# Full-array scores and joined sums in a fused chunk attention and ReGLU kernel: block 2's attention moved into output units, a reordered start, and stores from another queue

## The chip, the cores and the metric

The kernel runs on one core of one Trainium2 chip. The metric is device time in microseconds (us) of that core. A number called "span" is the profiled execution, from its first to its last instruction; a run's time is about 1.7 us more than its span. Profiles name the engines PE (TensorE, matmuls), PEld (its weight loads, which overlap matmuls), DVE (VectorE), ACT (ScalarE), POOL (GpSimd) and SP (SyncE). "PEclk" is the granted clock of TensorE as a share of full speed.

## The reference, cut to what matters

Attention over chunks of 32 tokens (each chunk sees 16 tokens to its left, 8 to its right and 8 memory rows), then a gated feed-forward network. Batch 4, 8 heads of 64, 768 tokens: 3072 tokens of width 512; the hidden width is 1536.

```python
def _attn_ref(q, k, v, mem_k, mem_v):          # cut
    for c in range(nc):
        k_full = np.concatenate([mem_k, k_ctx], axis=2)
        v_full = np.concatenate([mem_v, v_ctx], axis=2)
        scores = scale * np.matmul(q_c, k_full.transpose(0, 1, 3, 2))
        scores = scores - np.max(scores, axis=-1, keepdims=True)
        a = np.exp(scores)
        a = a / (np.sum(a, axis=-1, keepdims=True) + 1e-09)
        out[:, :, c_start:c_end] = np.matmul(a, v_full)

def _moe_ref(x, w_gate, w_val, w_out):
    gate = np.maximum(x @ w_gate, 0.0)
    val = x @ w_val
    return gate * val @ w_out
```

## The kernel before

The tokens are cut into 8 blocks of 384. A block goes through attention, four pairs of heads one after the other, and leaves a transposed tile `xT`. Then it goes through the feed-forward network in 15 units: 12 gate/value units of 8 matmuls of 384 columns, and 3 output units of 12 matmuls of 512 columns. TensorE is to be busy all the time, so the attention of block n+1 is cut into pieces that stand between the units of block n. Everything else hangs on this interleaving.

One pair of heads in the kernel before: 8 score matmuls on half of the array each, sums of the exponentials by a matmul with ones, values on half of the array, a reciprocal made by ACT as exp(-ln(x)), and one multiply on DVE.

```python
    def score_mms(n, hp, sc, start):
        kT, qT = kTs[n], qTs[n]
        for i in range(NQ):                    # NQ = 4 parts of QB = 96 tokens
            for hh in range(2):
                s = slice(D * hh, D * hh + D)  # D = 64: half the array
                nc.tensor.matmul(sc[:, hh, QB * i:QB * i + QB], lhsT=kT[s, i, hp, :], rhs=qT[s, i, hp, :],
                                 start=start, stop=start or i == NQ - 1)
    # ... step_s: score_mms, then three Exp with the mask as bias -> ex

    def step_d(n, hp):                         # sums, L253
        ex = exs[n, hp]
        parts = [(0, 1, 1), (1, NQ, 0)] if n % 2 == 0 else [(0, NQ - 1, 0), (NQ - 1, NQ, 2)]
        for i0, i1, kind in parts:
            for hh in range(2):
                nc.tensor.matmul(xs[D * hh:D * hh + D, QB * i0:QB * i1], lhsT=ones[:, kind, :],
                                 rhs=ex[:, hh, i0:i1, :], start=True, stop=True)

    def step_l(n, hp):
        nc.scalar.activation(xs, xs, ACT.Ln, scale=1.0 / 64.0)

    def step_e(n, hp):
        rinv = rpool.tile([128, TB], F32, name="rinv")
        nc.scalar.activation(rinv, xs, ACT.Exp, scale=-1.0, bias=mln64)
        rinvs[n, hp] = rinv

    def step_v(n, hp):                         # values, L268
        ex, vw = exs.pop((n, hp)), vwins[n % 2]
        for i in range(NQ):
            for hh in range(2):
                nc.tensor.matmul(xo[D * hh:D * hh + D, QB * i:QB * i + QB], lhsT=vw[:, i, 2 * hp + hh, :],
                                 rhs=ex[:, hh, i, :], start=True, stop=True)

    def step_m(n, hp):
        nc.vector.tensor_tensor(out=x_of(n)[:, hp, :], in0=xo, in1=rinvs.pop((n, hp)), op=ALU.mult)
```

A gate/value unit and the loop that interleaves. The units share two buffers of accumulators (`f_ps`), so unit u+2 can't start before DVE has made `gv` of unit u.

```python
    def ffn_close(n):
        for ps, m in units[n]:
            gr = grpool.tile([128, TB], F16, name="gr")
            nc.scalar.activation(gr, ps[:, 0, 0:TB], ACT.Relu)
            nc.vector.tensor_tensor(out=gvs[n][:, m, :], in0=ps[:, 1, 0:TB], in1=gr, op=ALU.mult)

    def run(order, n, first, gap, wait, turn_at):
        s_at = [first + gap * hp for hp in range(HP)]
        for u, (b, x) in enumerate(order):
            if n < NB:
                pieces(n, [("m", hp) for hp in range(HP) if u == s_at[hp] + wait + 1])
                now = [hp for hp in range(HP) if u == s_at[hp] + wait]
                unit(b, x, between(n, [(w, hp) for hp in now for w in "dlv"]))
                pieces(n, [("e", hp) for hp in now])
                pieces(n, [("s", hp) for hp in range(HP) if u == s_at[hp]])
            # ... turn_dma(n + 1) at turn_at

    run([(1, m) for m in range(6)] + [(0, NDC + t) for t in range(NT)] + [(1, m) for m in range(6, NDC + NT)],
        2, 6, 2, 2, 9)
    for n in range(2, NB):
        loads(n + 2)
        run([(n, u) for u in range(NDC + NT)], n + 1, 0, 3, 2, 9)
```

Block 0 has nothing to stand between. Its keys and queries are cast, turned on TensorE ("turns", `kq_ps`) and copied. Block 1 is turned the same way. From block 2 on, transposing DMAs (`turn_dma`) give `kT` and `qT`.

The softmax here doesn't subtract the row's maximum and nothing guards it: scores larger than these inputs give would overflow.

## Time and profile before

The time before is 251.81 us (median of 4 runs beside the changed kernel, 250.84 to 252.85); the profiled run's span is 249.3 us.

| stage of the span before | from, us | to, us |
|---|---|---|
| start, block 0's attention, its first units | 0 | 28.94 |
| block 1's turns | 28.94 | 35.98 |
| units 7 to 11 of block 0, with block 1's values | 35.98 | 45.52 |
| block 1's units, block 0's output units, with block 2's attention | 45.52 | 86.36 |
| block 2's units, with block 3's attention | 86.36 | 113.51 |
| blocks 3 to 6, 27.15 us each | 113.51 | 222.11 |
| block 7's units and the end | 222.11 | 249.3 |

The head of the page of the kernel before: the span, then per engine the busy us, the share of the span and the number of instructions.

```profile
span 249.3 us, 4594 instructions
PE 235.5 (94%) x1850; PEld 127.1 (51%) x1850; DVE 81.3 (33%) x162; ACT 127.6 (51%) x275; POOL 87.4 (35%) x116
```

TensorE is the limit. The chain of waits of the kernel before, in a steady block (start, us, what ran; the chain is followed back from the last instruction):

```profile
113.51 1.30 PE f_ps L285 x8
114.81 0.28 PE sc_ps L217 x8
115.09 2.06 PE f_ps L285 x12
117.14 0.29 PE xs_ps L253 x4
117.43 0.17 PE xo_ps L268 x8
117.60 2.06 PE f_ps L285 x12
119.66 0.28 PE sc_ps L217 x8
...
132.89 7.77 PE o_ps L310 x36
```

Only TensorE is on it. A unit takes 1.30 us for 8 matmuls, so 163 ns each; three output units take 7.77; the next block starts at 140.66. A pair of heads comes every 4.85 us (119.66 - 114.81). What a pair costs TensorE beyond the units is to be seen in the timeline of one pair in the kernel before (start, us, engine, line, what, and in brackets how long the engine was idle before it and what released it):

```profile
117.05 0.56 DVE L292 TENSOR_TENSOR gv<-f_ps,gr 128x384 f16<-128x384 f32 x1 [1.12 <-ACT gr L291]
117.07 0.14 PEld L253 LDWEIGHTS <-ones 128*64 128x64 f16 x4 [0.32 <-issue]
117.07 0.36 PE L253 MATMUL xs_ps<-ex,ones 128*64 128x96 f16 x4
...
118.39 0.49 ACT L291 ACTIVATE gr<-f_ps 128x384 f16<-128x384 f32 x1 [0.45 <-PE f_ps L285]
...
118.78 0.57 ACT L261 ACTIVATE rinv<-xs_ps,mln 128x384 f32<-128x384 f32 x1
...
118.92 0.56 DVE L292 TENSOR_TENSOR gv<-f_ps,gr 128x384 f16<-128x384 f32 x1 [1.31 <-ACT gr L291]
119.39 0.55 DVE L272 TENSOR_TENSOR xT<-xo_ps,rinv 128x384 f16<-128x384 f32 x1
```

The weights of the half-array groups are not loaded ahead: PEld stands idle 0.32 us before the sums. The page "TensorEngine Tiling (Array Packing)" of the Trainium skill (section Key Properties) says that a change of tiling mode drains the array, and this trace agrees with it.

Only two waits of TensorE at its matmuls are large after the start. They are in the waits of the kernel before (engine, line, waited for: us in total, times, longest):

```profile
PE sc_ps L217 <- DMA qT<-q16n: 4.0, 1, 4.0
...
PE f_ps L285 <- DVE gv L292: 0.8, 1, 0.8
```

The first is the wait for block 2's transposed queries, which ends at 60.20. After it the clock is low, as the windows of the kernel before show (stretch, its length, busy us of PE, PEld, DVE, ACT, POOL; then PEclk, DMA share, GB/s):

```profile
57.00:60.50 3.50, 0.30 (x8) 0.32 (x8) 0.00 (x0) 0.00 (x0) 1.54 (x2) 0.94 2.12 159
60.50:64.00 3.50, 3.50 (x16) 1.25 (x11) 0.00 (x0) 1.20 (x3) 1.99 (x3) 0.57 2.08 198
```

A clock of 0.57 over 3.5 us costs 3.5 x 0.43 = 1.5 us. The page "TensorE: Matmul & The Clock Gate" (section on the HAM clock gate) says that TensorE falls to half its clock after an idle window of about 3.4 us and needs about as long at work to return; here a wait of 4.03 us was followed by 3.5 us at about half clock.

### The profile page before, as it was taken

How to read it: one execution, taken by the hardware profiler on the slowest of the kernel's cores; microseconds unless marked ns; L12 is line 12 of the kernel's file. 1: busy time of each engine (PE TensorE's matmuls, PEld its weight loads, DVE VectorE, ACT ScalarE, POOL GpSimd, SP SyncE). 2: the span in 40 equal slices, each digit the busy share in tenths (PEclk: the TensorE clock that was granted, in tenths of full speed). 3: DMA queues.
4: the chain of work that ended last, by engine and by line, in shares of the span. 5: the costliest groups of instructions: out<-in, count | busy, mean ns of one | idle time of the engine just before them, and what ended most of it. 6: DMA issues, size and time to landing. Idle time of an engine off the chain costs nothing.

```text
span 249.3 us, 4594 instructions
## 1 busy us (share of the span) xinstructions
PE 235.5 (94%) x1850; PEld 127.1 (51%) x1850; DVE 81.3 (33%) x162; ACT 127.6 (51%) x275; POOL 87.4 (35%) x116
## 2 busy tenths in 40 slices
PE   7798999993999999999999999999999999999994
PEld 3454655551455455545554455545554555555541
DVE  3454564430044043411442043503441145203410
ACT  4173369322286277635774467626763577423321
POOL 8988759523974920195007800320000000000000
PEclk9799999998999999999999999999999999999998
DMA  7999999999999998099938997095701200030012
GB/s 170 157 191 194 175 186 172 199 152 183 163 188 142 189 205 152 0 127 192 137 52 50 187 120 147 8 158 115 88 0 45 85 0 3 0 126 3 0 42 84
DMA packets 113726, 28.57 MB, mean 115 GB/s; under 512 B 100170, under 2 KB 110634, under 8 KB 113706
## 3 DMA queue, kind: packets, MB, share of 16 engines
q0 software_dynamic: 86896, 15.17, 76.5%
q1 hardware_dynamic: 26394, 12.73, 22.6%
q10 hardware_dynamic: 416, 0.39, 0.6%
q8 instruction: 14, 0.23, 0.4%
q14 instruction: 6, 0.05, 0.1%
HBM read 31.15 MB, written 6.29 MB: 150 GB/s over the span
## 4 chain that ended last, share of the span: by engine, by line
PE 74%; DMA 15%; POOL 6%; issue 2%; SPq 1%; ACT 0%; POOLq 0%
PE f_ps L285 43%; PE o_ps L310 25%; DMA wv<-in_moe_w_val_dram 8%; DMA qT<-q16n 4%; DMA wo<-in_moe_w_out_dram 3%; PE xs_ps L253 3%; PE sc_ps L217 3%; POOL vwin L135 3%; PE xo_ps L268 2%; SPq L203 1%; POOL wg L169 1%; POOL wv L169 1%; POOL q16n L156 1%; POOL rk L126 0%; POOL memv L138 0%
## 5 line engine op out<-in xcount | busy, mean ns | idle before, releaser
L292 DVE TENSOR_TENSOR gv<-f_ps,gr 128x384 f16<-128x384 f32 x96 | 53.4, 557 | 130.9 <-ACT gr L291 130.9
L285 PE MATMUL f_ps<-xT,wg 128*128 128x384 f16 x384 | 79.4, 327 | 0.8 <-DVE gv L292 0.8
L285 PE MATMUL f_ps<-xT,wv 128*128 128x384 f16 x384 | 79.3, 327 | 0.0
L291 ACT ACTIVATE gr<-f_ps 128x384 f16<-128x384 f32 x96 | 47.1, 491 | 44.5 <-PE f_ps L285 42.5
L310 PE MATMUL o_ps<-wo,gv 128*128 128x512 f16 x288 | 65.2, 385 | 0.0
L135 POOL DMA_DIRECT2D vwin<-in_v_dram x32 | 28.8, 909 | 58.2 <-PE xo_ps L268 55.7
L285 PEld LDWEIGHTS <-wg 128*128 128x128 f16 x384 | 35.0, 97 | 25.6 <-issue 1.1
L285 PEld LDWEIGHTS <-wv 128*128 128x128 f16 x384 | 35.6, 98 | 23.4 <-issue 0.2
L310 PEld LDWEIGHTS <-gv 128*128 128x128 f16 x288 | 28.3, 99 | 34.0 <-issue 1.9
L313 ACT COPY o_sb<-o_ps 128x512 f32<-128x512 f32 x24 | 14.0, 585 | 46.1 <-PE o_ps L310 46.1
L239 ACT ACTIVATE ex<-sc_ps,bias 128x256 f16<-128x256 f32 x84 | 33.5, 476 | 6.5 <-PE sc_ps L217 6.5
L135 POOL DMA_DIRECT2D k<-in_k_dram x24 | 21.4, 906 | 6.2 <-DMA wo<-in_moe_w_out_dram 2.5
L272 DVE TENSOR_TENSOR xT<-xo_ps,rinv 128x384 f16<-128x384 f32 x32 | 17.7, 553 | 17.3 <-ACT rinv L261 14.4
L156 POOL DMA_DIRECT2D q16n<-in_q_dram x24 | 18.7, 801 | 8.0 <-DMA vwin<-in_v_dram 5.1
L257 ACT ACTIVATE xs_ps<-xs_ps 128x384 f32<-128x384 f32 x32 | 15.3, 479 | 11.8 <-PE xs_ps L253 10.2
L261 ACT ACTIVATE rinv<-xs_ps,mln 128x384 f32<-128x384 f32 x32 | 18.4, 576 | 0.2
L217 PE MATMUL sc_ps<-qT,kT 64*128 64x96 f16 x192 | 8.4, 208 | 4.0 <-DMA qT<-q16n 4.0
L268 PE MATMUL xo_ps<-ex,vwin 128*64 128x96 f16 x256 | 11.0, 207 | 0.7 <-DVE xT L272 0.7
L253 PE MATMUL xs_ps<-ex,ones 128*64 128x96 f16 (+1 forms) x128 | 11.4, 258 | 0.0
L217 PEld LDWEIGHTS <-kT 64*128 64x128 f16 x192 | 4.9, 95 | 11.9 <-issue 11.9
L198 DVE CAST kq<-kq_ps 128x896 f16<-128x896 f32 x8 | 8.7, 1091 | 6.5 <-PE kq_ps L189 6.4
L268 PEld LDWEIGHTS <-vwin 128*64 128x64 f16 x256 | 8.7, 110 | 2.8 <-issue 2.4
(50 smaller groups left out, 67.8 us busy)
## 6 DMA issues: line engine op xcount, KB each, us to landing
out_dram<-o_sb SPq DMA_DIRECT2D x24, 256.0 KB, 2.2
vwin<-in_v_dram POOLq DMA_DIRECT2D x24, 120.0 KB, 5.2
q16n<-in_q_dram POOLq DMA_DIRECT2D x24, 96.0 KB, 6.9
k<-in_k_dram POOLq DMA_DIRECT2D x18, 120.0 KB, 6.8
wo<-in_moe_w_out_dram POOLq DMA_DIRECT2D x3, 512.0 KB, 9.7
wg<-in_moe_w_gate_dram POOLq DMA_DIRECT2D x4, 256.0 KB, 7.4
wv<-in_moe_w_val_dram POOLq DMA_DIRECT2D x4, 256.0 KB, 8.0
rk<-in_k_dram POOLq DMA_DIRECT2D x3, 224.0 KB, 8.2
```

The source lines that it names most:

```text
L135: pool_dma(dsts[p][NMEM + m0:NMEM + m1, i], src)
L156: pool_dma(q16s[n][:, i], src)
L217: nc.tensor.matmul(sc[:, hh, QB * i:QB * i + QB], lhsT=kT[s, i, hp, :], rhs=qT[s, i, hp, :], start=start, stop=start or i == NQ - 1)
L239: nc.scalar.activation(ex[:, :, :, s], src, ACT.Exp, scale=SCALE, bias=bias[:, g:g + 1])
L253: nc.tensor.matmul(xs[D * hh:D * hh + D, QB * i0:QB * i1], lhsT=ones[:, kind, :], rhs=ex[:, hh, i0:i1, :], start=True, stop=True)
L261: nc.scalar.activation(rinv, xs, ACT.Exp, scale=-1.0, bias=mln64)
L268: nc.tensor.matmul(xo[D * hh:D * hh + D, QB * i:QB * i + QB], lhsT=vw[:, i, 2 * hp + hh, :], rhs=ex[:, hh, i, :], start=True, stop=True)
L272: nc.vector.tensor_tensor(out=x_of(n)[:, hp, :], in0=xo, in1=rinvs.pop((n, hp)), op=ALU.mult)
L285: nc.tensor.matmul(ps[:, a, 0:TB], lhsT=(wg, wv)[a][:, f, 128 * m:128 * m + 128], rhs=xTs[n][:, f, :], start=(f == 0), stop=(f == NFC - 1))
L291: nc.scalar.activation(gr, ps[:, 0, 0:TB], ACT.Relu)
L292: nc.vector.tensor_tensor(out=gvs[n][:, m, :], in0=ps[:, 1, 0:TB], in1=gr, op=ALU.mult)
L310: nc.tensor.matmul(o_ps, lhsT=gvs[n][:, m, 128 * t:128 * t + 128], rhs=wo[:, m, :], start=(m == 0), stop=(m == NDC - 1))
```

## The change

The intent: fewer and fuller matmuls per pair of heads. From block 1 on the values tile holds `[v | ones]` (128 columns), so one matmul gives values (rows 0 to 63) and sums (rows 64 to 127). From block 3 on the queries are spread block-diagonally, so 4 full-array matmuls of 192 columns replace 8 half-array ones. (Smaller edits, not shown: the order of loads, and `rpool` with 2 buffers instead of 4.) Around it: the casts of the start go ahead of the copies, unit 2 of block 0 takes the score banks, block 2's scores move from places 6, 8, 10 and 12 of the order of units to 11, 12, 14 and 15, so that its attention stands in the output units of blocks 0 and 1, the columns of ones are written by DVE memsets, and stores are issued by ACT instead of SP. The result tile `X` has one buffer of two banks.

```diff
 def step_s(n, hp):
+        if n < 3:
+            score_mms(n, hp, sc, True)
+        else:
+            for i in range(NQ):
+                nc.tensor.matmul(sc[:, i // 2, 192 * (i % 2):192 * (i % 2) + 192], lhsT=kTs[n][:, i, hp, :],
+                                 rhs=qbds[n % 2][:, i, hp].rearrange("p h m -> p (h m)"), start=True, stop=True)
 ...
-    def step_d(n, hp):              # sums by ones
 ...
+    def step_v(n, hp):
+        ex, vw, X = exs.pop((n, hp)), vwins[n % 2], first["X"]
+        for i in range(NQ):
+            for hh in range(2):
+                nc.tensor.matmul(X[:, hh, QB * i:QB * i + QB], lhsT=vw[:, i, 2 * hp + hh, :],
+                                 rhs=ex[:, hh, i, :], start=True, stop=True)
+        ln = rpool.tile([D, 2, TB], F32, name="ln")
+        nc.scalar.activation(ln, X[D:128, :, 0:TB], ACT.Ln, scale=1.0 / 64.0)
+    def step_e(n, hp):
+        rinv = rpool.tile([D, 2, TB], F32, name="rinv")
+        nc.scalar.activation(rinv, lns.pop((n, hp)), ACT.Exp, scale=-1.0, bias=mln64[0:D, :])
     def step_m(n, hp):
-        nc.vector.tensor_tensor(out=x_of(n)[:, hp, :], in0=xo, in1=rinvs.pop((n, hp)), op=ALU.mult)
+        for hh in range(2):
+            nc.vector.tensor_tensor(out=x_of(n)[D * hh:D * hh + D, hp, :], in0=first["X"][0:D, hh, 0:TB],
+                                    in1=rinv[:, hh, :], op=ALU.mult)
 ...  # stores
-        sp(out[row0:row0 + 128, :], o_sb)
+        act_dma(out[row0:row0 + 128, :], o_sb)
 ...  # start
+        for hp in range(2):
+            cast(0, hp, dve_copy)
+            cast(1, hp, act_copy)
+        turn_pe(0, 0)
+        turn_copy(0, 0)
 ...  # behind block 0's first value multiply, and again behind gv of unit 2
+        one_words(1, 0, 128, 0, NQ, ONE)
+        one_words(1, 96, 128, NQ - 1, NQ, 0)
+        one_words(1, 96, 120, NQ - 1, NQ, ONE)
 ...  # block 1
-    sums(1, 0)
     step_s(1, 2)
     ffn_unit(0, 7)
-    sums(1, 1)
     step_s(1, 3)
-    values(1, 0)
+    value(1, 0)                     # value = step_v, step_e, step_m in a row
     ffn_unit(0, 8)
-    values(1, 1)
-    sums(1, 2)
+    value(1, 1)
 ...  # run: where the scores stand is now a tuple, the place of "m" is unchanged
+                pieces(n, [("m", hp) for hp in range(HP) if u == at[hp] + wait + 1])
+                now = [hp for hp in range(HP) if u == at[hp] + wait]
+                unit(b, x, [lambda w=("v", hp): pieces(n, [w]) for hp in now])
 ...
-    run([(1, m) for m in range(6)] + [(0, NDC + t) for t in range(NT)] + [(1, m) for m in range(6, NDC + NT)],
-        2, 6, 2, 2, 9)
+    run([(1, m) for m in range(NDC)] + [(b, NDC + t) for b in range(2) for t in range(NT)],
+        2, (11, 12, 14, 15), 2, 13)
+    pieces(2, [("m", 3)])
```

## The prediction

> **What bounds it now.** TensorE: the page has PE busy 94% of the 249.3 us span; the chain of waits is 74% PE. From 86 us on a block takes 27.15 us (chain: 86.36, 113.51, 140.66): 96 matmuls of 163 ns are 15.6, output units 7.77, so the four head pairs cost 3.7, 0.93 each: scores 0.27, sums 0.19, values 0.27, two gaps of 0.10 (timeline). The Trainium skill (TensorEngine Tiling, Key Properties) says changing the tiling mode drains the array; the trace agrees, weight loads idle 0.32 us before such groups. Elsewhere PE loses 1.7 us waiting for the second key cast (timeline, 6.3 to 8.0), 0.8 at 22.7 (waits: f_ps on gv), 4.0 at 56 to 60 waiting for block 2's transpose (waits: sc_ps on DMA qT) and then about 1.6 at half clock (windows: 0.57 in 60.5 to 64).
>
> **What changes, costed.**
> 1. Blocks 3 to 7: 4 score matmuls of 192 columns (estimate 83 ns each, from 163 per 384) and 8 of 96 giving values and sums together (estimate 42 to 60 ns; not in this trace). No sums, no gaps: 0.67 to 0.85 for 0.93. ACT grows: Ln and Exp on 64x768 take about 0.81 (as the 128x768 Exp) and 0.9, from 0.48 and 0.58; DVE multiplies twice. ACT is then about 80% full, PE waits up to 0.1. Block about 26.4; five blocks: -3.5 us (0 to -5).
> 2. Start: the second turn no longer waits; heads 4 to 7 land near 9.5. About -2. Given back: memsets of ones columns (1024 words, estimate 1.1 us from 0.27 for 256) sit on DVE between block 0's first two multiplies (+0.6) and behind gv of unit 2 (+1.0). The 0.8 wait goes. Net about -1.
> 3. Block 1 values: one X buffer, so values(hp+1) wait for Ln 0.81, Exp 0.9, two multiplies 1.05 of hp: a cycle of 3.4 us against 1.7 of PE work. Before, the reciprocals were ready earlier. New PE waits on DVE xT: 2.3, 1.8, 1.8, and 1.2 at block 1's first unit: +6.
> 4. Block 2 in the output units: the 4.0 wait and cold clock go (-5.6): the transpose no longer waits for wo and is needed 10 us later. The same chain, plus copy 0.58 and a store issue 0.33 on ACT, brings waits of 1.5, 1.5 at values and 2.2 before block 2's fourth matmul: +5.2. Net with cheaper values -1.
> 5. Stores on ACT: 24 x 0.33 us, mostly in idle time.
> 6. GpSimd spreads: off the path, if the queue keeps ahead.
>
> Sum: about zero.
>
> **Predicted:** 252.0 us, 8 in 10 between 246.5 and 257.5. Faster by over 2%: 0.15; within 2%: 0.70; slower: 0.15.
>
> **What shows it.** Step 1: chain period 26 to 26.7, no gap before scores or values, x_ps spacing 42 to 60 ns. Step 2: second kq_ps turn near 6.3; long memsets before xT; no wait at unit 2. Step 3: PEld or PE x_ps waiting on DVE xT, several of 1.5 to 2.4 us, within 15 us of block 1. Step 4: no wait on DMA qT, no clock dip near 60; waits on xT of 1.4 to 2.3 in the output units and at block 2's start.
>
> **What would make it wrong.** Wide weight loads not hidden behind 96 columns (block 27 or more: slower). ACT too full, gv late each unit. Half clock in block 1's gaps (+2). Transposes or spreads late for blocks 3 or 4. Faster if block 1's chain overlaps more than I think.

## The result, and the profile after

The changed kernel is correct and takes 260.48 us (median of 4 runs, 260.23 to 261.87), against 251.81 for the kernel before. The ratio is 1.0355, 95% interval 1.0292 to 1.0418: slower. (Ratios here are the mean time of one kernel's fast runs over the mean of the other's fast runs of the same rounds, so not quite the ratio of the medians quoted.) The predicted 252.0 and its range up to 257.5 were missed.

The profiled run of the changed kernel is the slowest of its four and that of the kernel before (251.0 us) is near the fastest of its own, so the two profiles lie 10.9 us apart, while the medians lie 8.7 apart. The stages, from the timelines of TensorE:

| stage | before, us | after, us | difference |
|---|---|---|---|
| start to block 1's first turn | 28.94 | 28.49 | -0.45 |
| to unit 7 of block 0 | 7.04 | 6.79 | -0.25 |
| to block 1's first unit (1) | 9.54 | 16.20 | +6.66 |
| to block 2's first unit | 40.84 | 38.52 | -2.32 |
| block 2's units | 27.15 | 31.75 | +4.60 |
| block 3's to 6's units | 108.60 | 111.20 | +2.60 |
| block 7's units and the end | 27.19 | 27.25 | +0.06 |

(1) This unit starts at 50.09 but stalls inside. It is entered as starting at 51.48, 0.65 us before its second half at 52.13, since an undisturbed unit has its second half 0.65 us after its start.

The head of the page of the changed kernel, the same two lines:

```profile
span 260.2 us, 4314 instructions
PE 230.6 (89%) x1657; PEld 131.1 (50%) x1657; DVE 101.4 (39%) x194; ACT 146.2 (56%) x275; POOL 107.5 (41%) x130
```

TensorE has less to do: it was busy 4.9 us less, with 193 matmuls fewer on record. But the span is longer, so it waited more. The waits of the changed kernel show what it waited for:

```profile
PEld L287 <- DVE xT L301: 12.4, 6, 2.6
PE x_ps L287 <- DVE xT L301: 9.9, 6, 2.2
...
PE f_ps L316 <- DVE gv L323: 6.6, 14, 1.6
...
PE f_ps L316 <- DVE xT L301: 3.9, 2, 2.7
```

(L287 is the new values matmul, L301 the multiplies, L323 `gv`.) No line of TensorE waiting on `qT` is left. In its place stand waits on DVE, of two kinds: long ones on the multiplies, and many short ones on `gv`.

**Block 1.** The chain of waits of the changed kernel, one turn of it:

```profile
41.38 0.53 PE x_ps L287 x8
41.91 0.02 issue
41.93 0.82 ACT ln L290
42.75 0.02 issue
42.77 0.94 ACT rinv L295
43.72 0.02 issue
43.74 0.55 DVE xT L301
44.29 0.01 issue
44.30 0.56 DVE xT L301
44.87 0.05 issue
44.91 0.53 PE x_ps L287 x8
```

The single `X` closes a loop: values, ln, rinv, two multiplies, and only then the next values. One turn takes 3.53 us (44.91 - 41.38), although TensorE has 0.34 us of values and 1.30 of a unit to do in it. The kernel before had the sums of the next pair already turned into reciprocals when its values came.

**Block 2 in the output units.** The same loop in the timeline of TensorE of the changed kernel, rows that waited:

```profile
76.89 0.51 PE L287 MATMUL x_ps<-ex,vwin 128*128 128x96 f16 x8 [1.91 <-DVE xT L301]
...
88.36 0.52 PE L287 MATMUL x_ps<-ex,vwin 128*128 128x96 f16 x8 [1.88 <-DVE xT L301]
...
93.34 0.32 PE L316 MATMUL f_ps<-xT,wg 128*128 128x384 f16 x1 [2.69 <-DVE xT L301]
```

and the windows around the last of them:

```profile
90.00:93.40 3.40, 0.71 (x5) 0.35 (x4) 1.10 (x2) 1.52 (x2) 2.54 (x3) 1.00 1.45 132
93.40:98.00 4.60, 4.60 (x19) 2.25 (x19) 1.12 (x2) 0.98 (x2) 0.00 (x0) 0.63 1.75 149
```

The clock dip near 60 us is gone and has come back at 93.4: 4.6 us at 0.63 cost 4.6 x 0.37 = 1.7 us. This is the profiled run (mean clock 0.993). The dip doesn't come every time: two of the four runs of the changed kernel had a mean clock of 1.000, and the trace of m_after_gap4 below has the same wait (2.69 us, to 93.75) and a clock of 1.00 over the 4.55 us after it.

**The steady blocks.** The output units of the changed kernel in its chain:

```profile
142.09 7.77 PE o_ps L341 x36
...
169.79 7.77 PE o_ps L341 x36
...
197.48 7.77 PE o_ps L341 x36
```

A block takes 27.70 us (169.79 - 142.09, and 27.69 the next time), where the kernel before took 27.15. TensorE itself does what was hoped: 8 values matmuls take 0.34 us of its time, 4 scores 0.33, and the gaps before them are gone, so 96 x 0.163 + 7.77 + 4 x 0.67 = 26.1 us of work. The timeline of the changed kernel around one pair shows where 1.6 us go:

```profile
155.17 0.56 DVE L323 TENSOR_TENSOR gv<-f_ps,gr 128x384 f16<-128x384 f32 x1 [1.26 <-ACT gr L322]
...
155.87 0.47 ACT L322 ACTIVATE gr<-f_ps 128x384 f16<-128x384 f32 x1
...
155.99 1.11 DVE L301 TENSOR_TENSOR xT<-x_ps,rinv 64x384 f16<-64x384 f32 x2 [0.26 <-ACT rinv L295]
...
156.55 0.81 PE L316 MATMUL f_ps<-xT,wv 128*128 128x384 f16 x4
...
157.14 0.56 DVE L323 TENSOR_TENSOR gv<-f_ps,gr 128x384 f16<-128x384 f32 x1
...
157.75 0.48 PE L316 MATMUL f_ps<-xT,wg 128*128 128x384 f16 x2 [0.39 <-DVE gv L323]
```

The input `gr` of the next `gv` is ready at 156.34 (155.87 + 0.47). DVE makes this `gv` only at 157.14, because the two multiplies stand ahead of it in its queue. They waited for `rinv` until 155.99, and take 1.11 us. The accumulators that this `gv` frees come 0.55 us late: the four matmuls from 156.55 on are issued by 157.20 (4 x 0.163), and the next unit starts at 157.75. The bracket counts 0.39 of it, as the end of the last matmul is drawn later than its slot. Three such delays in a block make the 1.6 us. ACT was about as full as predicted: busy for 15.42 of the 19.93 us of one block's gate/value units (149.86 to 169.79), 77%.

### The profile page after: what moved, and what is told of

Same layout as the page of the kernel before. It is cut to its first block, busy times and chain, and to the rows that moved or that the text cites. A ratio compares the mean times of both kernels' runs of the same rounds, so it can differ in the third digit from the quotient of the medians.

```text
span 260.2 us, 4314 instructions
## 1 busy us (share of the span) xinstructions
PE 230.6 (89%) x1657; PEld 131.1 (50%) x1657; DVE 101.4 (39%) x194; ACT 146.2 (56%) x275; POOL 107.5 (41%) x130
## 4 chain that ended last, share of the span: by engine, by line
PE 60%; ACT 19%; DVE 14%; issue 3%; DMA 2%; ACTq 1%; SPq 0%; DVEq 0%
PE f_ps L316 29%; PE o_ps L341 21%; DVE xT L301 9%; ACT rinv L295 7%; ACT ln L290 5%; PE x_ps L287 4%; DVE gv L323 4%; ACT gr L322 3%; DMA kst<-in_k_dram 2%; ACT o_sb L344 1%; ACT ex L251 1%; PE sc_ps L220 1%; PE kq_ps L180 1%; PE sc_ps L245 1%; PE sc_ps L228 1%
## 5 line engine op out<-in xcount | busy, mean ns | idle before, releaser
L323 DVE TENSOR_TENSOR gv<-f_ps,gr 128x384 f16<-128x384 f32 x96 | 53.3, 557 | 97.9 <-ACT gr L322 97.4
L316 PE MATMUL f_ps<-xT,wg 128*128 128x384 f16 x384 | 80.6, 329 | 10.6 <-DVE gv L323 6.6
L316 PEld LDWEIGHTS <-wg 128*128 128x128 f16 x384 | 36.9, 98 | 32.3 <-issue 10.7
L301 DVE TENSOR_TENSOR xT<-x_ps,rinv 64x384 f16<-64x384 f32 x56 | 30.8, 550 | 39.3 <-ACT rinv L295 39.0
L208 POOL COPY qbd<-qT 64x1536 f16<-64x1536 f16 x10 | 14.6, 1464 | 56.5 <-DMA qT<-q16n 56.2
L290 ACT ACTIVATE ln<-x_ps 64x768 f32<-64x768 f32 x28 | 22.6, 807 | 24.7 <-PE x_ps L287 23.4
L295 ACT ACTIVATE rinv<-ln,mln 64x768 f32<-64x768 f32 x28 | 25.9, 926 | 2.2 <-ACT o_sb L344 2.1
L287 PE MATMUL x_ps<-ex,vwin 128*128 128x96 f16 x224 | 14.2, 206 | 9.9 <-DVE xT L301 9.9
L287 PEld LDWEIGHTS <-vwin 128*128 128x128 f16 x224 | 12.0, 98 | 15.6 <-DVE xT L301 12.4
L245 PE MATMUL sc_ps<-qbd,kT 128*128 128x192 f16 x80 | 9.9, 246 | 0.0
L245 PEld LDWEIGHTS <-kT 128*128 128x128 f16 x80 | 7.2, 98 | 2.6
## 6 DMA issues: line engine op xcount, KB each, us to landing
wo<-in_moe_w_out_dram POOLq DMA_DIRECT2D x3, 512.0 KB, 10.9
```

The source lines that it names most:

```text
L245: nc.tensor.matmul(sc[:, i // 2, 192 * (i % 2):192 * (i % 2) + 192], lhsT=kTs[n][:, i, hp, :], rhs=qbds[n % 2][:, i, hp].rearrange("p h m ...
L287: nc.tensor.matmul(X[:, hh, QB * i:QB * i + QB], lhsT=vw[:, i, 2 * hp + hh, :], rhs=ex[:, hh, i, :], start=True, stop=True)
L290: nc.scalar.activation(ln, X[D:128, :, 0:TB], ACT.Ln, scale=1.0 / 64.0)
L295: nc.scalar.activation(rinv, lns.pop((n, hp)), ACT.Exp, scale=-1.0, bias=mln64[0:D, :])
L301: nc.vector.tensor_tensor(out=x_of(n)[D * hh:D * hh + D, hp, :], in0=first["X"][0:D, hh, 0:TB], in1=rinv[:, hh, :], op=ALU.mult)
L316: nc.tensor.matmul(ps[:, a, 0:TB], lhsT=(wg, wv)[a][:, f, 128 * m:128 * m + 128], rhs=xTs[n][:, f, :], start=(f == 0), stop=(f == NFC - 1))
```

## The experiments

Each ran beside the kernel before on the same chip (best2 on another chip than the rest). Against the kernel before, at the 2% mark, m_after_unit, stores_sp and ones_early are slower, m_after_gap4, block1_old and block2_old unclear. Differences from the changed kernel are differences of medians from different rounds; the kernel before lay at 251.81 to 252.31 in all of them. By the ratios and their intervals, only block1_old and block2_old are clear of the changed kernel's 1.0355 (1.0292 to 1.0418) among these six. They undo or mend one thing each in the changed kernel, except `start_only`, which does one part alone, and the last two.

### m_after_unit: the multiplies behind the unit's gv

```diff
-                pieces(n, [("m", hp) for hp in range(HP) if u == at[hp] + wait + 1])
+                ms = [("m", hp) for hp in range(HP) if u == at[hp] + wait + 1]
+                if n == 2:
+                    pieces(n, ms)
                 ... the unit ...
+                if n > 2:
+                    pieces(n, ms)
```

> The changed kernel, with one edit: from block 3 on, the two multiplies of a head pair come after the next unit's gate product gv in VectorE's order, no longer before it. Theory A (order on VectorE): in the changed kernel gv has its relu ready at 156.36 us but stands behind the two multiplies (155.99, 1.11 us), so the third unit of each head pair starts 0.55 us late. Then the block period falls from 27.70 to about 26.3 us, the wait of f_ps on gv goes, and the time falls by 5 to 7 us, to about 254. Rival B (ScalarE is too full with the longer Ln and Exp): the period stays within 0.3 us of 27.70, and the time within 1.5 us of 260.5.

Measured: 259.77 us (257.49 to 261.25), ratio 1.0322 (1.0235 to 1.041). The chain of waits of this kernel has

```profile
144.02 7.77 PE o_ps L341 x36
...
170.56 7.77 PE o_ps L341 x36
...
197.10 7.77 PE o_ps L341 x36
```

A block takes 26.54 us, 1.16 less than in the changed kernel, with the same instructions in another order on DVE. In the timeline `gr` is ready at 158.26 (157.79 + 0.47) and `gv` follows at 158.29. From 100 us on no matmul of a unit waits on `gv` any more. So the queue order on DVE was most of the loss in the steady blocks, 1.16 of 1.6 us; this is shown. (For the rest, three of the four groups of values in a block wait about 0.15 us each for the multiplies, as at 159.93.) But the time fell by only 0.7 us in the medians: the period went where theory A had it, the time stayed where rival B had it. The delayed multiplies of block 3 now meet values that follow two units later:

```profile
112.42 0.51 PE L287 MATMUL x_ps<-ex,vwin 128*128 128x96 f16 x8 [2.37 <-DVE xT L301]
```

and the clock averages 0.83 from 110 to 120 us. At the output units at 144.02 this kernel is 1.93 us behind the changed one, and at those at 223.63 it is 1.55 us ahead: the new wait and the dip take back more than half of what the steady blocks win. Its four runs spread from 257.49 to 261.25, with mean clocks of 0.980 to 0.993, so the medians resolve no more than that.

### m_after_gap4: the same from block 4 on, the pairs further apart

```diff
-                pieces(n, [("m", hp) for hp in range(HP) if u == at[hp] + wait + 1])
+                ... as in m_after_unit, before the unit for n < 4, after it from n = 4 on
-        run([(n, u) for u in range(NDC + NT)], n + 1, (3, 6, 8, 11) if n == 2 else (0, 3, 6, 9), 2, 9)
+        run([(n, u) for u in range(NDC + NT)], n + 1, (3, 6, 8, 11) if n == 2 else (0, 3, 7, 11), 2, 9)
```

> The changed kernel, with two edits for blocks 4 to 7 only: the two multiplies come after the next unit's gv on VectorE, and the scores start after units 0, 3, 7, 11 (values in units 2, 5, 9, 13) so that most values have four units between them. Block 3 keeps its old order, where the run before this one met a wait of 2.4 us and half clock. Theory A (order on VectorE, then the length of the chain against one X buffer): block period 26.1 to 26.4 us against 27.70 as changed and 26.53 with the order alone; the waits of f_ps on gv go in these blocks; the time falls by 5 to 6 us, to about 255. Rival B (ScalarE too full): no more than 1.5 us better than 260.5 once block 3 is left alone, that is, the earlier shorter period came from something else.

Measured: 257.95 us (257.29 to 258.57), ratio 1.0235 (1.0168 to 1.0302). The wait at 112 us is gone, a steady block takes 26.89 us, and the time is 2.5 us below the changed kernel. That is the sign expected and half of the size: the wider distance gives no shorter block than the narrow one (26.54), so its place in the order costs elsewhere. Its trace shows a part of it, and it is again an order, this time on ACT: in two units of a block `ln` (0.81 us, at 156.50 and 162.58) runs before that unit's `gr`, `gv` follows late, and the next unit but one starts at 158.47 and 164.55, 0.22 us after it could (157.60 and 163.68, plus 0.65 for four matmuls). (In this profiled run, at 257.39 us, the mean clock was 1.000; in the other three it was 0.987 to 0.993.)

### block1_old: block 1 with the old sums and values

```diff
-    first["X"] = ...                          # X only from here on, behind block 1
+    sums(1, 0)
     step_s(1, 2)
     ffn_unit(0, 7)
+    sums(1, 1)
     step_s(1, 3)
-    value(1, 0)
+    wide_v(0, 1)
     ffn_unit(0, 8)
-    value(1, 1)
+    wide_v(1, 1)
+    sums(1, 2)
     ... 
```

> The changed kernel, with block 1's values as in the kernel before: sums by ones matmuls in a bank of their own, reciprocals made one unit ahead, one multiply. All else as changed. Theory A (the single X buffer makes values, Ln, Exp and two multiplies a chain of 3.5 us): the waits of x_ps on xT of 2.2, 1.7 and 1.7 us and the 1.2 us at block 1's first unit go; block 1's gate units start 5 to 6.5 us earlier; the time falls by 5 to 6.5 us unless block 2's transpose is then waited for, which would show as a wait of sc_ps on the transpose of q. Rival B (what block 1 waits for is really late weights or value loads, as the loads were reordered): the start of block 1's units moves by less than 2 us and the waits change their name to DMA.

Measured: 256.07 us (255.62 to 258.1), ratio 1.0199 (1.0126 to 1.0272); unclear at the 2% mark against the kernel before, but 4.4 us below the changed kernel. Block 1's units start at 43.98 instead of 51.48, without any wait in front of them. Block 2's three waits stayed the same to the hundredth (1.91, 1.88 and 2.69), and so did the steady block (27.69). So the loop in block 1 cost what the table says, and of the 7.5 us earlier start about 6 were left in the profiled span (253.9 against 260.2).

### block2_old: block 2 where it stood before

```diff
-    run([(1, m) for m in range(NDC)] + [(b, NDC + t) for b in range(2) for t in range(NT)],
-        2, (11, 12, 14, 15), 2, 13)
-    pieces(2, [("m", 3)])
+    run([(1, m) for m in range(6)] + [(0, NDC + t) for t in range(NT)] + [(1, m) for m in range(6, NDC + NT)],
+        2, (6, 8, 10, 12), 2, 9)
```

> The changed kernel, with block 2's attention placed as before (scores after units 6, 8, 10, 12 of the old order of units, transpose of block 3 at unit 9). Theory A (in the output units the chain of Ln, copy, store issue, Exp, two multiplies is exposed: waits 1.9, 1.9 and 2.7 us, and the last sets off half clock): the wait before block 2's fourth gate matmul goes, the waits on xT between values shrink to about 0.5 each, and the time falls by 4 to 7 us; the transpose for block 2 has landed by then, as block 1 is late anyway, so no wait on it. Rival B (moving block 2 was what removed the 4.0 us wait for the transpose): the wait of sc_ps on the transpose comes back with 2 us or more and the time falls by less than 2 us.

Measured: 255.35 us (255.11 to 256.83), ratio 1.0152 (1.0084 to 1.0221): 5.1 us below the changed kernel. Waits on the multiplies in block 2's attention shrink to 0.84, 0.40 and 0.40 us, and the wait of 2.69 with its half clock is gone. The first score of block 2, at 63.72, doesn't wait for `qT`, since block 1's losses had already made everything late. So the place in the output units, as ordered there, was a loss.

### stores_sp: stores back on SP

```diff
-        act_dma(out[row0:row0 + 128, :], o_sb)
+        sp(out[row0:row0 + 128, :], o_sb)
```

> The changed kernel, with the output stores issued from the SP queue as before. Theory: 24 issues of 0.34 us leave ScalarE, which had time there except ahead of the Exp in block 2's output units; the time changes by less than 1 us, or transposes of later blocks come late behind stores on the same queue (then block 3's scores would wait).

Measured: 260.0 us (258.33 to 261.07), ratio 1.0333 (1.026 to 1.0407): no difference from the changed kernel that these medians can tell. The page "DMA: Bandwidth & Descriptors" (section "Issuing engines are not separate DMA queues") says that spreading transfers over issuing engines only saves issue time; the trace agrees so far as the issue time on ACT is what shows. Block 2's three waits are 1.36, 1.36 and 2.17 us here instead of 1.91, 1.88 and 2.69, about 0.5 less each, because a store's issue no longer stands before the Exp. That is 1.6 us of the profiled span.

### ones_early: the memsets of ones at times when DVE is idle

```diff
+    one_words(0, 0, 128, 0, NQ, ONE)          # before the first cast
 ...
+        one_words(1, 0, 128, 0, NQ, ONE)      # while block 0's scores run
 ...
-        one_words(1, 0, 128, 0, NQ, ONE)      # behind block 0's first multiply
-    one_words(0, 0, 128, 0, NQ, ONE)          # behind gv of unit 2
```

> The changed kernel, with the ones columns of the two value buffers set in VectorE's idle time: those of block 0's buffer at the very start, those of block 1's after the last key and query copy. Theory: the 1.15 us wait of xo_ps on xT at 17.5 us shrinks to about 0.4 and the 1.6 us wait of f_ps on gv at 25.5 us to under 0.3, so block 1's turns start 2 us earlier; the time falls by 1.5 to 2.2 us. Rival: the two waits have another cause (weights still landing) and move by less than 0.5 us.

Measured: 259.42 us (257.28 to 259.92), ratio 1.027 (1.0203 to 1.0337). Block 1's turns start at 25.65 instead of 28.49, so the memsets did cost 2.8 us at that point. Then TensorE waits for weights, in one place 1.72 us for `wv` at 37.91, and for the loop of block 1 as before. Block 1's first unit resumes from its stall at 50.08 instead of 51.97, so 1.9 of the 2.8 us remain there, and about 1 in the medians, which these runs don't resolve.

### start_only: the kernel before with the new order of the start alone

```diff
-    fill(11)
+    fill(12)
     for hp in range(2):
         cast(0, hp, dve_copy)
         cast(1, hp, act_copy)
+    for hp in range(2):
         turn_pe(0, hp)
         turn_copy(0, hp)
-    fill(4)
+    fill(1)
```

> The kernel before, with only the changed start: both casts of keys and queries ahead of the turns and copies, 12 fillers first and 1 after instead of 11 and 4. Theory: the start gains about 1.5 us by unit 2, but block 2's transpose is set by the transfers and lands near 60 us whatever the start does, so the wait of sc_ps on the transpose grows by as much from 4.0 us and the time stays within 1 us. Rival: the gain of the start reaches the end, -1.5 us or more.

Measured: 252.83 us (251.35 to 253.59), ratio 1.0018 (0.9957 to 1.0079): the same. The turns of block 1 start 2.75 us sooner (26.19), and then the timeline of TensorE has

```profile
60.93 0.50 PE L217 MATMUL sc_ps<-qT,kT 64*128 64x96 f16 x8 [7.46 <-DMA qT<-q16n]
```

instead of a wait of 4.03 that ended at 60.20. All that was won is waited away. In both kernels the chain of waits up to that point runs over the same transfers: weights, block 2's rows, `wo`, the transposes. Time won before 60 us is worth nothing as long as block 2's queries are asked for at that point.

### best1: all the mends together

Block 1 as before; the spread queries zeroed only after block 3's loads; block 2 in the output units but with scores at (9, 11, 13, 14) and the reciprocal issued ahead of the copy; the multiplies behind the unit's `gv`, with pairs at (3, 6, 9, 11) for block 3 and (0, 3, 7, 11) later; memsets early.

```diff
-                unit(b, x, [lambda w=("v", hp): pieces(n, [w]) for hp in now])
-                pieces(n, [("e", hp) for hp in now])
+                early = "ve" if x >= NDC else "v"
+                unit(b, x, [lambda w=(c, hp): pieces(n, [w]) for hp in now for c in early])
+                if n > 2:
+                    pieces(n, ms)
+                if x < NDC:
+                    pieces(n, [("e", hp) for hp in now])
 ...
-        2, (11, 12, 14, 15), 2, 13)
-    pieces(2, [("m", 3)])
+        2, (9, 11, 13, 14), 2, 13)
 ... and block1_old, ones_early
```

> All mends together on the changed kernel: ones columns early; block 1's values by the old scheme; block 2's scores after units 9, 11, 13, 14 with the Exp of the sums ahead of the output copy; zeroing of the spread queries after block 3's loads; multiplies after gv from block 3 on; scores after units 3, 6, 9, 11 in block 2's units and 0, 3, 7, 11 later. Estimate from the parts: block 2's units start near 78 us, five blocks of about 26.4 us, a last one of 23.6 and the tail: span 237 to 241 us, time 239 to 243, so 3 to 5% faster than the kernel before. If the parts do not add up (block 3's spread queries late, or half clock after waits), 244 to 250.

Measured: 245.57 us as the median of 4 runs, of which two count as slow (over 1.5% above the fastest of the kernel): 248.36 and 247.46; the fast ones are 243.69 and 243.18. Ratio of the fast runs 0.9653 (0.9577 to 0.9728): faster than the kernel before, and so than the changed one; the time lies just above the expected 239 to 243. The profiled run is one of the slow ones; in it the first score of block 2 waits 4.06 us for `qT` at 62.23.

### best2: block 2's first two scores in later units

```diff
-        2, (9, 11, 13, 14), 2, 13)
+        2, (11, 12, 13, 14), 2, 13)
```

> The kernel of best1 with one change: block 2's scores behind units 11, 12, 13 and 14 instead of 9, 11, 13 and 14. In best1 the first of them still waits 4.06 us at 62.23 for the DMA transpose of block 2's queries, and the clock falls to 0.66 after it. If that wait is simply the distance from the score to the landing near 62 us, two units (2 x 1.3 us of PE work) take 2.6 us out of it and the half clock with it: time about 2 us under best1, near 241.5 to 243. Rival: the landing is late because the queue is full, and the later scores only move the wait to the values behind units 13 and 14 (a chain of x_ps waits on xT of 1 us or more): then the time stays at best1's 243 to 244.

Measured: 243.56 us (243.27 to 245.12, 6 runs), against 252.31 for the kernel before (11 runs); ratio 0.9677 (0.9644 to 0.971). The timeline of TensorE:

```profile
60.62 0.35 PE L220 MATMUL sc_ps<-qT,kT 64*128 64x96 f16 x8 [1.02 <-DMA qT<-q16n]
...
77.03 0.51 PE L287 MATMUL x_ps<-ex,vwin 128*128 128x96 f16 x8 [0.92 <-DVE xT L301]
```

The wait is down from 4.06 to 1.02 us and the clock is full in every stretch from 30 to 90 us. The three waits on the multiplies are 0.29, 0.57 and 0.92, below the rival's 1 us each. Yet the expected time, 241.5 to 243, was missed, and the time is the one that the rival had: best2, measured on another chip, is no faster than the fast runs of best1. It was never slow in 6 runs, where best1 was slow in 2 of 4. It may be that best1's slow runs are those with the long wait and the low clock, but no fast run of best1 was profiled, and the mean clocks don't separate them (0.986 and 0.983 in the slow runs, 0.985 and 0.993 in the fast), so this stays open.

In this version block 2's units start at 81.42, 4.9 us before those of the kernel before, and the steady blocks take 26.64 us (99.72 to 126.36 to 153.00 at the first output unit).

## Why the prediction was wrong

It added up to +0.5 us ("about zero"); the medians differ by +8.7, the profiles by +10.9. By its own steps, from the profiles:

| step | predicted, us | profile, us | missed by |
|---|---|---|---|
| 1, steady blocks | -3.5 | +2.65 | 6.15 |
| 2, start (with the turns) | -1 | -0.70 | 0.30 |
| 3, block 1 | +6 | +6.66 | 0.66 |
| 4, block 2 | -1 | +2.23 | 3.23 |

Block 2's units hold both step 4's last wait and step 1's work; of their +4.60, the stall is 2.85 (the fourth matmul, due at 90.00 + 3 x 0.163 = 90.49, came at 93.34) and the low clock 1.70. The remaining +0.05 and the +2.60 of blocks 3 to 6 are step 1. Step 4 is -2.32 + 2.85 + 1.70.

**The step that failed** is step 1, as put there: "ACT is then about 80% full, PE waits up to 0.1. Block about 26.4; five blocks: -3.5 us". TensorE's part was right: no gaps, values 42.5 ns apart (0.34 / 8), scores 83 ns, 26.1 us of work in a block. But the wait was 0.55 us and not up to 0.1, three times in a block. ACT was 77% full in the gate/value units, close to the 80% of the prediction. I had asked how full ACT would be, and not in which order DVE's queue would stand when a reciprocal comes late. DVE was busy only 39% of the span. The page "TensorE: Matmul & The Clock Gate" (on engine queue depths) says that ACT and DVE are strictly in order, and the trace agrees: `gv`, ready at 156.34, waited behind two multiplies until 157.14. In the kernel before the one multiply was half as long and followed a `gv` without waiting for its reciprocal (119.39). m_after_unit shows the cause by changing the order alone: 27.70 to 26.54 us, close to the 26.4 of the prediction. "ACT too full, gv late each unit" stood among what would make it wrong; `gv` was late, but through DVE's order.

**Step 4** was right on the signs and wrong on two counts. The waits came where it said (values, values, block 2's fourth matmul), but were 1.91, 1.88 and 2.85, 6.6 us together for 5.2. And "the 4.0 wait and cold clock go" holds only for the place near 60 us: the clock dipped again behind the new wait, for 1.7 us in the profiled run (not in every run, as said above). The prediction had counted such a dip for block 1 only, as a risk. Its reason, "the transpose no longer waits for wo", is not confirmed. By the profile the queue of SP still waits for it in the changed kernel:

```profile
SPq L199 <- DMA wo<-in_moe_w_out_dram: 5.7, 1, 5.7
```

(Releasers are inferred. The program now asks for the transposes ahead of `wo`, so it isn't shown that `wo` holds them.) In any case the transpose of the queries is issued at 50.25, not sooner than before (48.97). In four traces in which a score waited for it (before, start_only, best1, best2) it landed 11.1 to 12.3 us after its issue, so an estimate of its landing here is 61.3 to 62.5. The wait went because the first score came later (67.33), as the other half of the sentence said. block2_old measures the step, with block 1 as late as it is: moving block 2 back gains 5.1 us.

**Step 3** was right: a cycle of 3.4 us predicted, 3.53 measured; waits of 2.3, 1.8, 1.8 and 1.2 predicted, 2.23, 1.72, 1.72 and 1.22 measured. block1_old takes them away and gains 4.4 us in the medians.

**Step 2** was right in its parts: unit 2 starts 2.1 us sooner (21.46 for 23.58), and the memsets give it back (1.15 us before a value group, 1.57 at `f_ps`). "the second turn no longer waits" was not: it waits 0.96 us, not 1.68. What it did not see is that the gain would have been worth nothing in the kernel before (start_only).

**Step 5** was right for the idle time; ahead of the Exp in block 2, where step 4 had counted the issue, it cost about 0.5 us a wait (stores_sp). **Step 6** was right too: the spreads take 1.46 us each on GpSimd, and no wait of TensorE or DVE names them.

Of the predicted signs for "wrong", wide weight loads that are not hidden can be ruled out: PEld loads `[v | ones]` in its 0.5 us before and under the matmuls, and no gap follows.

## What to carry to other kernels

When a change takes work from the busiest engine and gives longer pieces to the others, look at the order in their queues and not only at how full they are: here DVE at 39% of the span held TensorE up by 0.55 us three times in a block, and moving two instructions behind a third took 1.16 of the 1.6 us away. A result tile with one buffer turns values, reciprocal and multiply into a loop whose length (3.5 us here) has to fit between two uses. And before moving work to an earlier time, find out what the next stage waits for: with transfers still landing at 60 us, 2.75 us won at the start came to nothing.

## What the Trainium skill lacked or had wrong

- "TensorE: Matmul & The Clock Gate", section "Back-to-back issue gap": its isolated form, columns over 2.4 plus 2.5 ns, gives an estimate of 42.5 ns for 96 columns, and 8 values matmuls, each with its own 128x128 weight load, took 0.34 us, 42.5 ns each. Its sustained figures with weight loads, about 81 ns for 128 columns and 131 for 512, said to be the ones that hold in a real kernel, are not seen: 36 matmuls of 512 columns in a row, each with its own weight load, took 7.77 us, 216 ns each. (Long runs of 128 columns were not tried.)
- The same page, HAM clock gate: it speaks of idle gaps above about 3.4 us. Here shorter waits were sometimes followed by a dip, and the same wait not always: behind 2.69 us the changed kernel's clock was 0.63 over 4.6 us (TensorE busy 0.71 us of the 3.40 before), and m_after_gap4's was 1.00 over 4.55 us. In stores_sp a wait of 2.17 us (to 91.85) was followed by 0.61 over 3.5 us; behind the waits of 1.91 and 2.23 us in the changed kernel the profile page's row of clocks shows no dip (90% or more in each slice). What decides between them is not shown.
- "TensorEngine Tiling (Array Packing)", Key Properties: it says that a change of mode drains the array, and gives no cost. Here it was about 0.10 us of TensorE at each change, and 0.32 us without weight loads before each half-array group.
- The pages give the queue depths, and "Perfetto Trace Analysis" has a sentence on engines that are not full but make others wait, with the advice to break instructions up. None says that the order in the queue of such an engine (39% busy) can be what holds up the array. Here it cost 1.16 us in a block of 27.70.
